# Causal attention with a three-way maxout FFN on one core: high and low halves of the probabilities in one interleaved tile, one DMA transpose per query block, and a new list of matmul counts

## The chip, the cores and the metric

The kernel runs on one core of a Trainium2 chip. Its time is the device time of one execution in microseconds (us). Three runs of the kernel before gave 855.0, 856.35 and 856.51; the median, 856.35, is the time that the changed kernel is compared with. Engines are named as in the profile: PE is TensorE (PEld its weight loads), DVE is VectorE, ACT is ScalarE, POOL is GpSimd, SP is SyncE, which here only issues DMAs.

## The reference, cut to what matters

Eight batches, eight heads, 576 tokens, head size 64. Attention is causal with a bias from a running sum, and its output goes through a maxout FFN:

```python
scores = scale * np.matmul(q, k.transpose(0, 1, 3, 2))
cum = np.cumsum(np.maximum(s, 0.0), axis=-1)
bias = -(cum[:, :, :, None] - cum[:, :, None, :])
scores = np.where(causal, -1000000000.0, scores + np.minimum(bias, 0.0))
attn = np.exp(scores - np.max(scores, axis=-1, keepdims=True))
attn = attn / (np.sum(attn, axis=-1, keepdims=True) + 1e-09)
x = np.matmul(attn, v)          # -> tokens x 512
h = np.maximum(np.maximum(x @ w1, x @ w2), x @ w3)      # 512 -> 768
out = h @ w_out                                          # 768 -> 512
```

## The kernel before, in words

Two heads (j = 0, 1) are worked on together; four such pairs make a batch. The 576 queries of a pair are cut into blocks 0 to 3 of 128 and block 4 of 64 (there the two heads share one tile of 128 rows). A *step* is one block of one pair; 160 steps follow one another. Steps 0 to 15 are blocks 0 and 1 of the first two batches, steps 16 to 39 their blocks 2, 3 and 4, and steps 40 to 159 take the other six batches, five blocks a pair.

Numbers that need more than 16 bits of precision are held as a high half (the value rounded to f16) and a low half (what is left). In step t:

- `scores` (L430, L443, L473, L490) makes the scores of step t+2 on PE in one of two PSUM tiles `s`. It can start only when step t has finished reading its own tile.
- `highest` (L513 or L518, DVE) takes the row maximum, `expo` (L535, ACT) the exponentials and their sums, `inverse` (L548, DVE) 1/sum.
- `probs` makes the high half on ACT (L592, tile `prh`) and the low half on DVE (L595, tile `prl`), the last reader of `s`. For steps 0 to 7 PE transposes both halves through PSUM (L600). In all later steps SP issues DMA transposes: blocks 0 to 3 one of `prh` into `ph` and one of `prl` into `pl` (L607), block 4 two of each (L614). `prh` and `prl` have two buffers each, so the high half of step t+2 waits for the transposes of step t.
- `values` (L674) multiplies with v a step later: 12 matmuls (`av`) for blocks 0 and 1 of a pair, 28 for blocks 2 to 4. They stand on PE ahead of the scores of the next step but one, first all that read `ph`, then those that read `pl`.

The FFN is cut into groups of matmuls: 18 groups of 12 (L810, tile `pm`) and 4 of 18 (L853, tile `po`) for each half of a batch, 256 or 320 tokens wide. A group can be issued when the attention output of that half batch is made. Groups wait in a queue, and from step 10 the list `PLAN` says how many FFN matmuls are issued in each step: the first number ahead of the scores of step t+2, the second behind them. The numbers are upper limits: where the queue is empty, `run_some` issues nothing.

```python
        if fine:
            run_some(PLAN[t - FINE][0])
        ...
        if t + 2 < len(steps):
            scores(t + 2)
        ...
        if fine:
            run_some(PLAN[t - FINE][1])
        ...
        if due:
            values(*due.pop(0))
```

All loads of q, k and v from step 16 on, the output stores and the transposes stand in one queue on SP, in program order.

Of the kernel before, what the change touches and what calls it, by code (L numbers as in the profile page):

```python
# [8 lines left out]
F32 = mybir.dt.float32  # L9
F32R = mybir.dt.float32r  # L10
F16 = mybir.dt.float16
# [10 lines left out]
def kernel(  # L22
# [9 lines left out]
    nc = tc.nc  # L32

    P = 128
    D = 64
    B, NP, _, QKV = qkv.shape
    HB, S = s.shape
# [8 lines left out]
    Q4 = 4 * P  # L46
# [5 lines left out]
    PH = [(0, 256), (256, 320)]  # L52
# [3 lines left out]
    NSEC = 0.417  # L56
    FINE = 10
    PLAN = [
# [13 lines left out]
    ]  # L72

    const = ctx.enter_context(tc.tile_pool(name="const", bufs=1))
# [1 line left out]
    io = ctx.enter_context(tc.tile_pool(name="io", bufs=1))  # L76
    att = ctx.enter_context(tc.tile_pool(name="att", bufs=2))
# [4 lines left out]
    ps_m = ctx.enter_context(tc.tile_pool(name="ps_m", bufs=3, space=PSUM))  # L82
# [118 lines left out]
    def load_w(i, dma=None):  # L201
# [12 lines left out]
        out=tri, in_=tri, pattern=[[-1, P]], compare_op=ALU.is_ge, fill=NEG, base=0, channel_multiplier=1  # L214
# [23 lines left out]
    identh = att.tile([P, P], F16, tag="q4", name="identh")  # L238
# [17 lines left out]
    def cumulate(part):  # L256
        c0, c1, a0, a1 = CUT[part]
        if part == 0:
            C["r"] = io.tile([HB, S], F32, tag="rv1", name="r_t")
            C["c"] = att.tile([HB, S], F32, tag="pTh1", name="c_t", bufs=1)  # L260
            C["cc"] = att.tile([HB, 2, S], F32R, tag="pTl1", name="cc", bufs=1)
            C["cn"] = const.tile([HB, 2, 6], F32R, name="cn")
        r, c, cc, cn = (C[x] for x in ("r", "c", "cc", "cn"))
        w = slice(c0, c1)
        if part == 0:
            nc.vector.tensor_scalar(out=r[:, w], in0=s_t[:, w], scalar1=0.0, scalar2=None, op0=ALU.max)
        nc.vector.tensor_tensor_scan(
            out=c[:, w], data0=r[:, w], data1=r[:, w], initial=c[:, c0 - 1:c0] if part else 0.0,
            op0=ALU.add, op1=ALU.max,
        )  # L270
        if part == 0:
            nc.vector.tensor_copy(out=cc[:, 0, w], in_=c[:, w])
        else:
            nc.scalar.activation(out=cc[:, 0, w], in_=c[:, w], func=AF.Copy)
        eng = nc.gpsimd if part else nc.vector
        eng.tensor_tensor(out=cc[:, 1, w], in0=c[:, w], in1=cc[:, 0, w].bitcast(F32), op=ALU.subtract)
        cf = cc.bitcast(F32)
        for a, x in (
            (slice(0, 2), slice(64, 2 * P, P)), (slice(2, 4), slice(2 * P + 64, Q4, P)),
            (slice(4, 6), slice(Q4 + 32, Q4 + 34)),  # L280
        ):
            if a0 <= a.start < a1:
                eng.tensor_scalar(out=cn[:, :, a], in0=cf[:, :, x], scalar1=-1.0, scalar2=None, op0=ALU.mult)

    C = {}
# [264 lines left out]
    PT = {}  # L550
    TP = {}

    def turned(t):
        tp, pT, m, i = TP.pop(t)
        for c in range(2):
            to, of = pT[c][:, 0:2 * m, i:i + P], tp[:, c, 0:2 * m, :]
            if c and t >= 2 * NP - 2:
                nc.vector.tensor_copy(out=to, in_=of)
            else:
                nc.scalar.activation(out=to, in_=of, func=AF.Copy)  # L560

    def probs(t):

        v, qb = steps[t]
        ps, nm, nk = U.pop(t)
        if t not in RI:
            inverse(t)
        se, nj = SE.pop(t)
        ph = 0 if qb < 2 else 1
        if qb in (0, 2):  # L570
            PT[v, ph] = [
                att.tile([P, (4 + 4 * ph, 4 + 6 * ph)[c], PH[ph][1]], F16, tag=f"pT{'hl'[c]}{ph}", name=f"p{'hl'[c]}{t}", bufs=1)
                for c in range(2)
            ]
        pT = PT[v, ph]
        ri = RI.pop(t)
        halves = [att.tile([P, 8, P], F16, tag=f"pr{c}", name=f"pr{c}{t}") for c in "hl"]
        if nj == 2:
            m = qb + 1
            i = (qb - 2 * ph) * P  # L580
            hv, lv = (x[:, 0:2 * m, :].rearrange("p (m j) c -> p m j c", j=2) for x in halves)
            sets = [
                (hv[:, :, j, :], lv[:, :, j, :], ps[:, j].rearrange("p (m c) -> p m c", c=P), ri[:, j:j + 1])
                for j in range(2)
            ]
        else:
            tail = halves[1][:, 4, :]
            hv, lv = (x[:, 0:4, :] for x in halves)
            src = ps[:, 0:Q4].rearrange("p (m c) -> p m c", c=P)
            sets = [(hv, lv, src, ri[:, 0:1]), (tail[:, 0:D], tail[:, D:P], ps[:, Q4:S], ri[:, 0:1])]  # L590
        for hi, lo, src, sc in sets:
            nc.scalar.activation(out=hi, in_=src, func=AF.Copy, scale=sc)  # L592
        yield
        for hi, lo, src, sc in sets:
            nc.vector.scalar_tensor_tensor(out=lo, in0=src, scalar=sc, in1=hi, op0=ALU.mult, op1=ALU.subtract)  # L595
        if v < NP:
            tp = ps_m.tile([P, 512], F32, tag="m", name=f"tp{t}").bitcast(F16).rearrange("p (c n k) -> p c n k", c=2, k=P)
            for c in range(2):
                for n in range(2 * m):
                    nc.tensor.transpose(out=tp[:, c, n, :], in_=halves[c][:, n, :], identity=identh)  # L600
                if c == 0:
                    for f, a in between.get(t, ()):
                        f(*a)
            TP[t] = (tp, pT, m, i)
        elif nj == 2:
            for c in range(2):
                nc.sync.dma_start_transpose(  # L607
                    out=pT[c][:, 0:2 * m, i:i + P], in_=halves[c][:, 0:2 * m, :].rearrange("p n c -> p (n c)")
                )
        else:  # L610
            for c in range(2):
                n = 4 + c
                for j in range(2):
                    nc.sync.dma_start_transpose(  # L614
                        out=pT[c][:, 0:2 * n, 256:320].rearrange("p (n j) c -> p n j c", j=2)[:, :, j, :],
                        in_=halves[c][j * D:(j + 1) * D, 0:n, :].rearrange("p n c -> p (n c)"),
                    )
        yield


# [34 lines left out]
    def values(v, ph):  # L655
        b, g, _ = visits[v]
        r = R[v]
        nq = PH[ph][1]
        pT = PT.pop((v, ph))
# [3 lines left out]
        for t in range(2):  # L663
            for kb in range(min(blocks[-1] + 1, 4)):
                c0 = max(kb - blocks[0], 0) * P
                for vt in ("vh", "vl")[:2 - t]:
                    for j in range(2):
                        todo.append((j, r[vt][:, j, kb, :], pT[t][:, 2 * kb + j, c0:nq], c0))
        if ph:
            for vt in ("vh", "vl"):  # L670
                for j in range(2):
                    todo.append((j, r[vt][:, j, 4, :], pT[1][:, 8 + j, 256:320], 2 * P))
        for n, (j, lt, rt, c0) in enumerate(todo):
            nc.tensor.matmul(  # L674
                av[j * D:(j + 1) * D, c0:nq], lhsT=lt, rhs=rt,
# [246 lines left out]
    todo = {}  # L922
# [253 lines left out]
```

## Time and profile before

| | |
|---|---|
| median of three runs | 856.35 us |
| profiled execution | 857.01 us, of which the span of instructions is 855.2 us |
| PE busy | 816.1 us (95%), granted clock 0.993 over the span |
| DVE, ACT, POOL busy | 555.9, 556.9, 417.1 us (65%, 65%, 49%) |
| DMA transposes | 368, in one queue with the loads and stores |

PE is busy nearly throughout, so the time is PE's work plus PE's idle time. The span begins with an attention stage in which the FFN queue is still short, and ends with FFN work alone. Matmuls overlap, and the duration of a single one is longer than the distance to the next; the rate is read from merged rows (so many matmuls in so many us).

### The profile page before, as it was taken

How to read it: one execution, taken by the hardware profiler on the slowest of the kernel's cores; microseconds unless marked ns; L12 is line 12 of the kernel's file. 1: busy time of each engine (PE TensorE's matmuls, PEld its weight loads, DVE VectorE, ACT ScalarE, POOL GpSimd, SP SyncE). 2: the span in 40 equal slices, each digit the busy share in tenths (PEclk: the TensorE clock that was granted, in tenths of full speed). 3: DMA queues.
4: the chain of work that ended last, by engine and by line, in shares of the span. 5: the costliest groups of instructions: out<-in, count | busy, mean ns of one | idle time of the engine just before them, and what ended most of it. 6: DMA issues, size and time to landing. Idle time of an engine off the chain costs nothing. (4 is left out here: it accounts for less than half of the span.)

```text
span 855.2 us, 19957 instructions
## 1 busy us (share of the span) xinstructions
PE 816.1 (95%) x7100; PEld 639.7 (75%) x7100; DVE 555.9 (65%) x1451; ACT 556.9 (65%) x1493; POOL 417.1 (49%) x621
## 2 busy tenths in 40 slices
PE   4988899997999999999999999999999999999998
PEld 3766677765677778777887788777887788777875
DVE  8978979676778667676766676666756675661110
ACT  4767768776687777777777676777766676651111
POOL 6513523234545657664756757464656656221221
PEclk9989999999999999999999999999999999999999
DMA  9823745896777686868777686657847565321000
GB/s 354 338 73 80 140 109 124 175 183 146 154 174 164 157 153 147 173 133 168 150 166 156 147 178 150 140 134 154 162 131 153 129 155 136 92 66 45 19 9 31
DMA packets 233668, 120.76 MB, mean 141 GB/s; under 512 B 209376, under 2 KB 218208, under 8 KB 233568
## 3 DMA queue, kind: packets, MB, share of 16 engines
q1 hardware_dynamic: 232416, 117.65, 60.2%
q10 hardware_dynamic: 1152, 1.84, 0.6%
q8 instruction: 56, 0.92, 0.5%
q14 instruction: 44, 0.36, 0.2%
HBM read 60.18 MB, written 9.44 MB: 81 GB/s over the span
## 5 line engine op out<-in xcount | busy, mean ns | idle before, releaser
L810 PE MATMUL pm<-x,w 128*128 128x256 f16 (+1 forms) x3456 | 456.6, 287 | 4.7 <-DVE x L684 2.8
L810 PEld LDWEIGHTS <-w 128*128 128x128 f16 x3456 | 326.9, 98 | 98.5 <-issue 12.7
L818 POOL CAST hh<-m 128x256 f16<-128x256 f32 (+1 forms) x96 | 50.2, 523 | 296.0 <-DVE m L829 227.5
L595 DVE SCALAR_TENSOR_TENSOR prl<-s,ri,prh 128x512 f16<-128x512 f32 (+3 forms) x288 | 152.7, 567 | 48.2 <-ACT prh L592 27.5
L592 ACT ACTIVATE prh<-s,ri 128x512 f16<-128x512 f32 (+3 forms) x288 | 141.7, 538 | 64.2 <-DVE ri L548 58.1
L535 ACT ACTIVATE s<-s,nm 128x512 f32<-128x512 f32 (+4 forms) x288 | 151.2, 525 | 24.9 <-DVE nm L513 14.4
L829 DVE SCALAR_TENSOR_TENSOR m<-pm,m 128x256 f32<-128x256 f32 (+1 forms) x192 | 87.1, 454 | 116.4 <-PE pm L810 94.1
L853 PE MATMUL po<-hh,w 128*128 128x256 f16 (+1 forms) x768 | 149.9, 287 | 0.0
L513 DVE CUSTOM_DVE_ANT_0 s<-s,later 128x128 f32<-128x128 f32 (+4 forms) x216 | 113.8, 527 | 43.1 <-PE s L430 23.7
L853 PEld LDWEIGHTS <-w 128*128 128x128 f16 x1152 | 109.5, 98 | 28.7 <-issue 1.7
L853 PE MATMUL po<-hl,w 128*128 128x320 f16 (+1 forms) x384 | 109.9, 286 | 0.0
L826 ACT ACTIVATE m<-pm 128x256 f32<-128x256 f32 (+1 forms) x96 | 38.8, 404 | 59.5 <-PE pm L810 57.4
L819 POOL TENSOR_TENSOR hl<-m,hh 128x256 f16<-128x256 f32 (+1 forms) x96 | 72.6, 757 | 7.8
L185 POOL TENSOR_TENSOR l<-raw,h 64x576 fp32r<-64x576 f32 x48 | 67.5, 1407 | 6.8 <-ACT h L172 5.9
L177 POOL TENSOR_TENSOR h<-raw,h 64x640 fp32r<-64x640 f32 x40 | 61.6, 1539 | 15.6 <-ACT h L168 15.0
L863 ACT ACTIVATE o<-po,os 128x256 f32<-128x256 f32 (+1 forms) x64 | 31.9, 499 | 55.5 <-PE po L853 54.7
L674 PEld LDWEIGHTS <-vh 128*64 128x64 f16 x832 | 45.3, 109 | 24.1 <-issue 18.0
L683 ACT ACTIVATE x<-av 128x256 f16<-128x256 f32 (+1 forms) x64 | 26.3, 410 | 54.4 <-PE av L674 54.3
L535 ACT ACTIVATION_READ_ACCUMULATOR s<-s,nm 128x1 f32 x288 | 57.2, 199 | 0.0
L430 PE MATMUL s<-h 128*128 128x128 f32 (+1 forms) x192 | 56.3, 369 | 0.8 <-ACT s L535 0.8
L155 POOL CAST l<-kb 64x576 fp32r<-64x576 f32 x48 | 32.8, 684 | 46.5 <-PE s L443 45.8
L548 DVE RECIPROCAL ri<-se 128x2 f32<-128x2 f32 (+1 forms) x160 | 25.4, 159 | 39.9 <-ACT se L540 39.2
(155 smaller groups left out, 1117.5 us busy)
## 6 DMA issues: line engine op xcount, KB each, us to landing
raw<-in_qk_dram SPq DMA_DIRECT2D x48, 608.0 KB, 4.4
r<-in_w_dram SPq DMA_DIRECT2D x24, 512.0 KB, 10.2
rv<-in_qkv_dram SPq DMA_DIRECT2D x32, 320.0 KB, 3.5
out_dram<-o SPq DMA_DIRECT2D x32, 160.0 KB, 2.0
out_dram<-o SPq DMA_DIRECT2D x32, 128.0 KB, 1.9
raw<-in_qkv_dram SPq DMA_DIRECT2D x8, 480.0 KB, 4.1
ph<-prh SPq DMA_TRANSPOSE x184, 3.0
pl<-prl SPq DMA_TRANSPOSE x184, 2.8
```

The costliest lines, as they stand in the source:

```text
L177: (nc.vector if v < 5 * NP else nc.gpsimd).tensor_tensor(out=h[own, 0:QP], in0=raw[own, 0:QP], in1=h[own, 0:QP].bitcast(F32), op=ALU.subtract)
L185: nc.gpsimd.tensor_tensor(out=l[far, QP:V0], in0=raw[far, QP:V0], in1=h[far, QP:V0].bitcast(F32), op=ALU.subtract)
L430: nc.tensor.matmul(ps[:, j, :nk], lhsT=w[:, qs], rhs=w[:, QP:QP + nk], start=(x == "h"), stop=(x == "l"), skip_group_check=True,)
L513: nc.vector.tensor_tensor_reduce(out=of, in0=of, in1=mask, scale=-SCALE, scalar=3.0e38, op0=ALU.add, op1=ALU.min, accum_out=nm[:, j:j + 1],)
L535: nc.scalar.activation(out=sc, in_=sc, func=AF.Exp, bias=nm[:, j:j + 1], scale=-1.0 if below(t) else 1.0, accum_out=sm[:, j:j + 1],)
L592: nc.scalar.activation(out=hi, in_=src, func=AF.Copy, scale=sc)
L595: nc.vector.scalar_tensor_tensor(out=lo, in0=src, scalar=sc, in1=hi, op0=ALU.mult, op1=ALU.subtract)
L810: nc.tensor.matmul(pm[:, :nq], lhsT=w[:, wt, kt, :], rhs=xt, start=(n == 0), stop=(n == 3 * NKT - 1))
L818: nc.gpsimd.tensor_copy(out=st["hh"][:, ft, :nq], in_=m1[:, :nq])
L819: nc.gpsimd.tensor_tensor(out=st["hl"][:, ft, :nq], in0=m1[:, :nq], in1=st["hh"][:, ft, :nq], op=ALU.subtract)
L829: nc.vector.scalar_tensor_tensor(out=m1[:, :nq], in0=pm[:, :nq], scalar=HSC, in1=m1[:, :nq], op0=ALU.mult, op1=ALU.max)
L853: nc.tensor.matmul(pm[:, :nq], lhsT=W[18 + ft][:, wt, dt, :], rhs=st[ht][:, ft, :nq], start=(n == 0), stop=(n == 3 * NFT - 1),)
```

## The change

**Tiles.** `prh` and `prl` become one tile `pr` of 16 blocks of 128 columns; for key block k it holds the high half of both heads, then the low half of both heads. `ph` and `pl` become one tile `pT` in the same order. Blocks 0 to 3 of a pair get one DMA transpose of twice the length, block 4 two (one for each head's 64 rows) in place of four: 184 transposes in place of 368, with the same data. In steps 0 to 7 the PE transposes are the same in number and order. The matmuls of `values` are the same, in the same order; all of them now read `pT`. The tile of the running sum (`c`) moves to another pool.

**The list.** `PLAN` is made anew.

```diff
     PLAN = [
-        (15, 0), (18, 12), (18, 12), (11, 1), (17, 16), (18, 12), (12, 0), (13, 17), (18, 12), (9, 0), (18, 9), (10, 14),
+        (24, 0), (18, 12), (18, 12), (19, 0), (17, 16), (18, 12), (18, 0), (9, 21), (19, 11), (15, 0), (14, 13), (12, 12),
 ...
@@ def probs(t):
-            PT[v, ph] = [
-                att.tile([P, (4 + 4 * ph, 4 + 6 * ph)[c], PH[ph][1]], F16, tag=f"pT{'hl'[c]}{ph}", name=f"p{'hl'[c]}{t}", bufs=1)
-                for c in range(2)
-            ]
+            PT[v, ph] = att.tile([P, 8 + 10 * ph, PH[ph][1]], F16, tag=f"pT{ph}", name=f"pt{t}", bufs=1)
         pT = PT[v, ph]
         ri = RI.pop(t)
-        halves = [att.tile([P, 8, P], F16, tag=f"pr{c}", name=f"pr{c}{t}") for c in "hl"]
+        pr = att.tile([P, 16, P], F16, tag="pr", name=f"pr{t}")
         if nj == 2:
-            hv, lv = (x[:, 0:2 * m, :].rearrange("p (m j) c -> p m j c", j=2) for x in halves)
+            both = pr[:, 0:4 * m, :].rearrange("p (m c j) k -> p m c j k", c=2, j=2)
             sets = [
-                (hv[:, :, j, :], lv[:, :, j, :], ps[:, j].rearrange("p (m c) -> p m c", c=P), ri[:, j:j + 1])
+                (both[:, :, 0, j, :], both[:, :, 1, j, :], ps[:, j].rearrange("p (m c) -> p m c", c=P), ri[:, j:j + 1])
                 for j in range(2)
             ]
 ...
         elif nj == 2:
-            for c in range(2):
-                nc.sync.dma_start_transpose(
-                    out=pT[c][:, 0:2 * m, i:i + P], in_=halves[c][:, 0:2 * m, :].rearrange("p n c -> p (n c)")
-                )
+            nc.sync.dma_start_transpose(
+                out=pT[:, 0:4 * m, i:i + P],
+                in_=pr[:, 0:4 * m, :].rearrange("p n c -> p (n c)"),
+            )
         else:
-            for c in range(2):
-                n = 4 + c
-                for j in range(2):
-                    nc.sync.dma_start_transpose(
-                        out=pT[c][:, 0:2 * n, 256:320].rearrange("p (n j) c -> p n j c", j=2)[:, :, j, :],
-                        in_=halves[c][j * D:(j + 1) * D, 0:n, :].rearrange("p n c -> p (n c)"),
-                    )
+            for j in range(2):
+                nc.sync.dma_start_transpose(
+                    out=pT.rearrange("p (k j) q -> p k j q", j=2)[:, :, j, 256:320],
+                    in_=pr[j * D:(j + 1) * D, 0:9, :].rearrange("p n c -> p (n c)"),
+                )
```

What the new list does on PE is read from the order of its instructions. Up to the scores of step 23 nothing moves. After that these are the FFN matmuls that stand between the scores of the step before and the scores of the step named (the largest differences):

```
ahead of the scores of step   24  27  30  32  33  35  36  39  42  44 | 57  58  59  60
before                        24  23  24  35  21  19  23  22  21  26 | 23  18  22  26
now                           33  31  30  40  26  25  30  29  24  30 | 13   0   0  21
```

At the scores of step 56 the new order has issued 55 FFN matmuls more than the old one, at those of step 60 as many. After that the two stay within 10 matmuls of each other.

On PE, at the scores of step 58 (`s`, four of 512 columns) in the kernel before; `po_1_2` is an FFN group, `w` its weights:

```order
L853 LDWEIGHTS w_2026
L853 MATMUL po_1_2_4596<-hh_1_3932,w_2026 128x320
L430 MATMUL s_4606<-h_0_3997 128x512
L430 MATMUL s_4606<-h_1_4194 128x512
L430 MATMUL s_4606<-l_0_3998 128x512
L430 MATMUL s_4606<-l_1_4195 128x512
L853 LDWEIGHTS w_2026
L853 MATMUL po_1_2_4596<-hh_1_3932,w_2026 128x320
```

The same place on PE in the changed kernel; `av` is the product with v of the pair before, `s_4500` the scores of step 58, `s_4527` those of step 59:

```order
L672 LDWEIGHTS vl_4081
L672 MATMUL av_1_4461<-pt_4234,vl_4081 64x64
L430 MATMUL s_4500<-h_0_3939 128x512
L430 MATMUL s_4500<-h_1_4135 128x512
L430 MATMUL s_4500<-l_0_3940 128x512
L430 MATMUL s_4500<-l_1_4136 128x512
L443 MATMUL s_4527<-h_0_3939 128x256
L443 MATMUL s_4527<-h_1_4135 128x256
```

No FFN matmul stands any more from the scores of step 57 to the `av` behind those of step 59; the queue is empty there.

On SP, from the load of a head (`raw`) in step 32 to the first transposes of step 34, before:

```order
L139 DMA raw_0_2852<-in_qk_dram 128x1216
L607 DMA_TRANSPOSE ph_2806<-prh_2883 128x8x128
L607 DMA_TRANSPOSE pl_2807<-prl_2884 128x8x128
L614 DMA_TRANSPOSE ph_2806<-prh_2954 128x4x64 x2
L614 DMA_TRANSPOSE pl_2807<-prl_2955 128x5x64 x2
L607 DMA_TRANSPOSE ph_3021<-prh_3023 128x6x128
L607 DMA_TRANSPOSE pl_3022<-prl_3024 128x6x128
```

And the same stretch of SP in the changed kernel, up to the load behind the first transpose of step 34:

```order
L139 DMA raw_0_2814<-in_qk_dram 128x1216
L606 DMA_TRANSPOSE pt_2763<-pr_2845 128x16x128
L612 DMA_TRANSPOSE pt_2763<-pr_2914 128x9x64 x2
L606 DMA_TRANSPOSE pt_2975<-pr_2976 128x12x128
L127 DMA rv_3028<-in_qkv_dram 128x640
```

Eight issues became four; each now stands behind the low half, where the one of `prh` stood behind the high half alone.

## Rows read from the trace of the kernel before

**Rows 1.** Busy us (x instructions) by stage; last three columns: PE clock, DMA share, GB/s.

```profile
0.00:130.00 130.00, 107.21 (x945) 83.53 (x945) 107.86 (x250) 87.66 (x249) 55.19 (x90) 0.96 0.61 183
130.00:262.00 132.00, 121.54 (x1064) 91.77 (x1060) 98.69 (x210) 96.13 (x241) 53.24 (x79) 1.00 0.75 159
262.00:760.00 498.00, 496.48 (x4356) 393.66 (x4355) 330.90 (x953) 355.94 (x967) 291.82 (x424) 1.00 0.67 146
760.00:856.00 96.00, 90.84 (x744) 70.76 (x742) 18.42 (x42) 17.13 (x39) 16.85 (x30) 0.99 0.12 33
```

**Rows 2.** PE's waits from 130 to 262 us: total, times, longest.

```profile
PE av L674 <- DMA pl<-prl: 3.9, 4, 2.2
PE s L490 <- DVE prl L595: 3.5, 4, 1.4
PE s L490 <- DVE am L342: 1.1, 1, 1.1
PE s L443 <- DVE prl L595: 1.0, 1, 1.0
PE s L430 <- ACT s L535: 0.8, 1, 0.8
```

**Rows 3.** Chain that ended last: start, us, what (its FFN matmuls alone).

```profile
781.14 23.58 PE pm L810 x216
...
812.72 29.34 PE pm L810 x216
```

**Rows 4.** Timeline, steps 32 to 39: start, us, engine, what, [idle before and releaser].

```profile
188.68 2.48 SPq L614 DMA_TRANSPOSE ph<-prh  x2
...
191.27 2.49 SPq L614 DMA_TRANSPOSE pl<-prl  x2
...
192.31 0.36 PE L490 MATMUL s<-qkh 128*128 128x256 f32 x1 [1.08 <-DVE prl L595]
...
196.23 0.65 PE L674 MATMUL av<-pl,vh 128*64 128x320 f16 x8 [1.35 <-DMA pl<-prl]
...
213.25 0.65 PE L674 MATMUL av<-pl,vh 128*64 128x320 f16 x8 [2.21 <-DMA pl<-prl]
```

**Rows 5.** Waits of the whole span: total, times, longest.

```profile
ACT prh L592 <- DMA ph<-prh: 5.3, 4, 2.8
...
PE av L674 <- DMA pl<-prl: 4.9, 5, 2.2
```

**Rows 6.** Transposes of line L607: issue on SP, ns min/median/max; issue to landing.

```profile
L607 SPq DMA_TRANSPOSE pl<-prl x120: 1167/1220/4210, 58.3 to 765.8; - x120
...
DMA to landing us min/median/max: 2.3/3.0/6.6
```

**Rows 7.** Scores of step 56 to those of step 60, columns as in Rows 1.

```profile
286.07:304.35 18.28, 17.47 (x151) 13.10 (x150) 11.44 (x30) 13.91 (x37) 11.42 (x17) 1.00 0.75 173
```

**Rows 8.** Timeline of that stretch: low halves of steps 56, 58; scores 58; FFN.

```profile
292.03 0.88 DVE L595 SCALAR_TENSOR_TENSOR prl<-s,ri,prh 128x256 f16<-128x256 f32 x2
...
294.60 0.74 PE L430 MATMUL s<-h 128*128 128x512 f32 x2
...
301.44 1.41 DVE L595 SCALAR_TENSOR_TENSOR prl<-s,ri,prh 128x512 f16<-128x512 f32 x2 [0.67 <-ACT prh L592]
...
303.24 1.36 PE L810 MATMUL pm<-x,w 128*128 128x256 f16 x11 [0.81 <-DVE x L684]
```

**Rows 9.** PE idle, and the granted clock behind it, columns as in Rows 1.

```profile
50.00:52.00 2.00, 0.34 (x4) 0.17 (x3) 1.90 (x9) 1.32 (x4) 0.77 (x2) 1.00 0.34 41
52.00:54.00 2.00, 1.78 (x12) 1.27 (x12) 0.45 (x2) 1.94 (x8) 1.54 (x3) 0.51 0.55 221
54.00:56.00 2.00, 2.00 (x16) 1.36 (x16) 1.64 (x4) 0.83 (x3) 0.00 (x0) 0.63 0.03 8
211.00:213.25 2.25, 0.04 (x2) 0.00 (x0) 0.60 (x1) 0.48 (x1) 1.06 (x1) 1.00 0.79 268
213.25:216.00 2.75, 2.75 (x28) 2.21 (x27) 2.07 (x4) 1.97 (x5) 0.00 (x0) 1.00 0.92 150
```

More of the change, by code (lines that the diff above doesn't have):

```diff
@@ L259, in cumulate @@
             C["r"] = io.tile([HB, S], F32, tag="rv1", name="r_t")
-            C["c"] = att.tile([HB, S], F32, tag="pTh1", name="c_t", bufs=1)
-            C["cc"] = att.tile([HB, 2, S], F32R, tag="pTl1", name="cc", bufs=1)
+            C["c"] = io.tile([HB, S], F32, tag="rv2", name="c_t")
+            C["cc"] = att.tile([HB, 2, S], F32R, tag="pT1", name="cc", bufs=1)
             C["cn"] = const.tile([HB, 2, 6], F32R, name="cn")
@@ L555, in turned @@
         for c in range(2):
-            to, of = pT[c][:, 0:2 * m, i:i + P], tp[:, c, 0:2 * m, :]
+            to = pT[:, 0:4 * m, i:i + P].rearrange("p (m c j) q -> p m c j q", c=2, j=2)[:, :, c]
+            of = tp[:, 0:4 * m, :].rearrange("p (m c j) k -> p m c j k", c=2, j=2)[:, :, c]
             if c and t >= 2 * NP - 2:
@@ L586, in probs @@
         else:
-            tail = halves[1][:, 4, :]
-            hv, lv = (x[:, 0:4, :] for x in halves)
+            both = pr[:, 0:8, :].rearrange("p (m c) k -> p m c k", c=2)
             src = ps[:, 0:Q4].rearrange("p (m c) -> p m c", c=P)
-            sets = [(hv, lv, src, ri[:, 0:1]), (tail[:, 0:D], tail[:, D:P], ps[:, Q4:S], ri[:, 0:1])]
+            sets = [
+                (both[:, :, 0, :], both[:, :, 1, :], src, ri[:, 0:1]),
+                (pr[:, 8, 0:D], pr[:, 8, D:P], ps[:, Q4:S], ri[:, 0:1]),
+            ]
         for hi, lo, src, sc in sets:
@@ L596, in probs @@
         if v < NP:
-            tp = ps_m.tile([P, 512], F32, tag="m", name=f"tp{t}").bitcast(F16).rearrange("p (c n k) -> p c n k", c=2, k=P)
+            tp = ps_m.tile([P, 512], F32, tag="m", name=f"tp{t}").bitcast(F16).rearrange("p (n k) -> p n k", k=P)
             for c in range(2):
-                for n in range(2 * m):
-                    nc.tensor.transpose(out=tp[:, c, n, :], in_=halves[c][:, n, :], identity=identh)
+                for n in (4 * k + 2 * c + j for k in range(m) for j in range(2)):
+                    nc.tensor.transpose(out=tp[:, n, :], in_=pr[:, n, :], identity=identh)
                 if c == 0:
@@ L605, in probs @@
         elif nj == 2:
-            for c in range(2):
+            nc.sync.dma_start_transpose(
+                out=pT[:, 0:4 * m, i:i + P],
+                in_=pr[:, 0:4 * m, :].rearrange("p n c -> p (n c)"),
+            )
+        else:
+            for j in range(2):
                 nc.sync.dma_start_transpose(
-                    out=pT[c][:, 0:2 * m, i:i + P], in_=halves[c][:, 0:2 * m, :].rearrange("p n c -> p (n c)")
-                )
-        else:
-            for c in range(2):
-                n = 4 + c
-                for j in range(2):
-                    nc.sync.dma_start_transpose(
-                        out=pT[c][:, 0:2 * n, 256:320].rearrange("p (n j) c -> p n j c", j=2)[:, :, j, :],
-                        in_=halves[c][j * D:(j + 1) * D, 0:n, :].rearrange("p n c -> p (n c)"),
-                    )
+                    out=pT.rearrange("p (k j) q -> p k j q", j=2)[:, :, j, 256:320],
+                    in_=pr[j * D:(j + 1) * D, 0:9, :].rearrange("p n c -> p (n c)"),
+                )
         yield
@@ L667, in values @@
                     for j in range(2):
-                        todo.append((j, r[vt][:, j, kb, :], pT[t][:, 2 * kb + j, c0:nq], c0))
+                        todo.append((j, r[vt][:, j, kb, :], pT[:, 4 * kb + 2 * t + j, c0:nq], c0))
         if ph:
@@ L671, in values @@
                 for j in range(2):
-                    todo.append((j, r[vt][:, j, 4, :], pT[1][:, 8 + j, 256:320], 2 * P))
+                    todo.append((j, r[vt][:, j, 4, :], pT[:, 16 + j, 256:320], 2 * P))
         for n, (j, lt, rt, c0) in enumerate(todo):
```

24 rows, old and new, of the table PLAN are left out of this document.

## The prediction

> **What bounds the kernel now.** I read the table of busy time by stage first. PE is idle 22.8 us up to 130 us, 10.5 from 130 to 262, 1.5 from 262 to 760 and 4.4 after that, and at full clock from 130 us on [rows 1]. From 262 us the kernel is PE's work and nothing else. The change neither adds nor takes away a matmul, so the time can only move through PE's idle time, and up to the scores of step 23 (about 130 us) the order on PE is as it was. What can be won is therefore the 10.5 us of steps 24 to 49 and about 1 us at the end; everything else can only be lost. The waits say who ends the 10.5 us [rows 2]: 6.4 us are scores that wait for their PSUM tile or its chain (3.5 + 1.1 + 1.0 + 0.8), 3.9 us are `av` matmuls that wait for the transposes of the low half. One FFN matmul costs PE 23.58 / 216 = 0.109 us at 256 columns and 29.34 / 216 = 0.136 us at 320 [rows 3].
>
> **Filler ahead of the scores.** Where PE waits for the attention chain, the scores start no earlier with more filler ahead of them, but the FFN matmuls moved there cost nothing. Steps 24 and 30 get 9 and 6 matmuls of 256 columns more, 0.98 and 0.65 us, inside waits of 1.4 and 1.1. Steps 42 and 44 get 3 and 4 of 320, 0.41 and 0.54, inside 0.8 and 1.0. For steps 33, 36 and 39, which with step 24's 1.4 make up the 3.5 us, the extra matmuls are as long as the waits or longer (7 of 320 are 0.95 us; step 36 waits 1.08 [rows 4] and has 6 more a step earlier), so all of 3.5 - 1.4 = 2.1 us goes. Sum: 0.98 + 0.65 + 0.41 + 0.54 + 2.1 = 4.7 us. Bounds: 0 if the filler only pushes the chain, 6.4 if the chain gains as well. I take -4.7.
>
> **Transposes.** An issue takes SP 1.22 us, and a transfer lands 3.0 us after its issue begins [rows 6]. At step 33 four issues follow each other from 188.68 to 193.76, and `av` waits until 196.23 [rows 4]. Now there are two, behind the low half. The merged issue and its landing stand in no row: the issue lies between 1.2 (as now) and 2.4 us (two of now), the landing between 2.3 and 4.2 us (3.0 and one issue more). I take 1.3 and 3.4, near the single issue, since its median barely differs from its minimum over tiles of 2 to 8 blocks. Two issues of 2.5 us together go from the path, so the wait of 1.35 us all but goes. In return the part of `av` that read the high half, about 1.0 us of PE work, cannot run ahead any more, so of the 2.21 us at 213.25 some 1.0 stays. With the two small waits that is 1.2 + 1.2 + 0.3: I take -2.7, between 0 and -3.9. At the end of the attention the same wait is 4.9 - 3.9 = 1.0 us [rows 2, 5], and ten more FFN matmuls now stand ahead of it in that step: -0.8, between 0 and -1.0.
>
> The Trainium skill (DMA: Bandwidth & Descriptors, Issuing engines are not separate DMA queues) holds that the time a sequencer takes to start a DMA is usually small beside the DMA itself. Here it is 1.22 of 3.0 us; by the page's rule this term would be near nothing and the sum 2.7 us longer.
>
> **What is paid for it.** At the scores of step 56 the new order has 55 matmuls more behind it, 55 x 0.136 = 7.5 us. They are missing in steps 56 to 59, where the queue is empty. Before, these four steps took 18.28 us with PE busy 17.47 [rows 7]; now PE has 10.0 us of work there, and the attention chain sets the pace. Its length is read from the same steps. From the scores of step 56 (286.07) to the end of its low half (292.91) are 6.84 us, then come the scores of step 58; from those (294.60) to the end of their low half (302.85) 8.25 us, then the scores of step 60 [rows 7, 8]: 15.1 us. On PE the 21 matmuls ahead of step 60 also wait for the output of `av`, as they do now at 303.24, and 12 or so of 0.109 us follow that wait: 16.0 us in all. Bounds for these four steps: 11.4 us, DVE's busy time there [rows 7], and 18.3 as now. With 16.0 the stretch gets only 2.3 us shorter for 7.5 us of work taken out of it: +5.2 us (bounds +0.6 and +7.5).
>
> The PE idles twice there, for about 1.6 and 2.9 us. In the trace an idle stretch of this length was once followed by a fallen clock: from 50 to 52 us PE is busy 0.34 us at full clock, and in the next four us the granted clock is 0.51 and 0.63, mostly the lower of the two levels (1.2 of 2.4 GHz); but after the 2.2 us at 211 it stays at 1.00 [rows 9]. At the price of that fall, (0.49 + 0.37) x 2 = 1.7 us, and an even chance, +0.9 us. The Trainium skill (TensorE: Matmul & The Clock Gate, HAM oscillation) says that PE falls back to its slow clock when it is left idle between bursts, which makes the next burst pay; by that alone the term is +1.7, and the row at 211 us shows an idle stretch that did not.
>
> **Later steps.** From step 61 to 159 PE waits 1.5 us in all [rows 1], so there is next to nothing to win. The new list takes up to 10 matmuls (1.4 us) from ahead of single scores and puts them behind, at about a dozen steps; a chain that just kept up then shows as a wait of some tenths. No row has it: between 0 and 3.5 us (12 x 0.3), I take +1.5.
>
> **Sum.** -4.7 - 2.7 - 0.8 + 5.2 + 0.9 + 1.5 = -0.6 us against the profiled execution, 857.01 us (855.2 of span and 1.8 around it): 856.4. That execution lies 0.66 above the median of the three runs, so against the median of 856.35 I say 855.7. Written with x for the length of steps 56 to 59, the sum is x - 17.5, and x is 16.0 + 0.9 in it.
>
> **Rivals.**
> *The stalls go and the empty queue costs little.* All 6.4 + 3.9 + 1.0 us of waits go, the later steps cost 0.3, the clock stays up, and the four steps take 16.0: -11.3 + 0.3 + 5.2 = -5.8, so 850.6 against the median. For it: both edits attack just these waits. Against it: scores held by the chain are held by DVE and ACT, which do the same work.
> *The empty queue decides (slower).* Steps 57 to 59 are left to a chain with PE idle; the chain gets no shorter than it was, and the clock falls: x = 18.3 + 1.7 = 20.0, sum +2.5, so 858.9 against the median; with 3.5 for the later steps 860.9. It decides for slower from x = 19.2 on. For it: ACT is busy 13.9 of 18.3 us there already [rows 7]. Against it: with fewer FFN evictions ACT and DVE are freer.
> *The one tile holds the chain.* The high half of step t+2 now waits for both halves' transposes of step t, where it waited for those of `ph` alone; that was already 5.3 us in four places [rows 5], all before 215 us where loads crowd the queue. If each becomes 1 us longer and the scores follow, it is +4 on the -0.6: 859.8. Against it: with half the issues the merged transfer should land no later than the second of now.
>
> **Chances.** The forecast 0.46 (its own range 853.7 to 857.9), the stalls gone 0.27, the empty queue 0.20, the one tile 0.07. A change under 0.2%, 1.7 us, cannot be told from none here. Of the forecast's 0.46, 0.09 is faster and 0.04 slower than that. Faster: 0.27 + 0.09 = 0.36; the same: 0.33; slower: 0.20 + 0.07 + 0.04 = 0.31. The range, 851.0 to 860.0, leaves out the far ends of the two large rivals.
>
> **What would show it.** In the profile after: PE's waits before the scores of steps 24 to 44 should sum to about 1.7 us, those of `av` for transposes to about 1.2. Between the scores of steps 56 and 60 there should be 16 to 17 us with PE busy about 10 to 11, and two idle stretches of 1.5 to 3 us ahead of the scores of steps 58 and 59, with DVE's low half as releaser. The issue of a merged transpose should be near 1.3 us. I am wrong in the main term if the four steps take under 14 or over 18.3 us, in the second if `av` still waits 3 us or more, and in the last if PE idles more than 4 us from 310 to 760 us.

## The result

Slower by 0.7%: the changed kernel took 861.95 us (four runs, 861.72 to 862.32) against 856.13 for the kernel before in the same comparison. The ratio is 1.0071 (95% interval 1.0053 to 1.0088). Timed again, with six runs, it was 1.0063 (1.0039 to 1.0087). The forecast was no change, with slower at 0.31; the time lies above the range.

Up to the scores of step 23 both traces run alike (129.14 and 129.28 us), so everything below is counted from there to the end of the span: 726.1 us before, 730.8 after. The table of busy time by stage after, which answers [rows 1] (stage, length, then busy us and instructions of PE, PEld, DVE, ACT, POOL, last PE clock, DMA share, GB/s):

```profile
0.00:130.00 130.00, 106.76 (x943) 83.42 (x945) 108.11 (x250) 87.52 (x249) 54.63 (x90) 0.96 0.57 182
130.00:262.00 132.00, 126.50 (x1101) 95.91 (x1098) 97.91 (x209) 95.57 (x238) 55.26 (x81) 0.99 0.74 158
262.00:760.00 498.00, 490.80 (x4277) 388.79 (x4277) 331.01 (x948) 354.44 (x960) 288.37 (x419) 0.99 0.66 146
```

PE idles 5.5 us from 130 to 262 us, where it was 10.5: half of it is won. From 262 to 760 it idles 7.2 us, where it was 1.5. The sum of PE's busy time grew as well, by 3.7 us (816.1 to 819.8) for the same matmuls: the granted clock fell twice behind step 23. Cut at the same steps in both kernels, first before, then after (scores of step 23 to those of 45, to those of 60, to the end):

```profile
129.14:239.64 110.50, 100.23 (x889) 76.11 (x888) 81.82 (x165) 79.64 (x196) 44.89 (x65) 1.00 0.74 156
239.64:304.35 64.71, 63.70 (x530) 47.45 (x529) 48.40 (x128) 50.61 (x137) 36.08 (x53) 1.00 0.78 169
304.35:855.23 550.88, 545.78 (x4751) 433.30 (x4748) 318.08 (x910) 339.78 (x917) 281.71 (x417) 1.00 0.57 125
```

```profile
129.28:242.18 112.90, 107.40 (x942) 81.99 (x941) 81.73 (x165) 81.21 (x202) 45.25 (x65) 0.98 0.73 156
242.18:306.08 63.90, 59.45 (x477) 44.12 (x476) 46.98 (x128) 49.00 (x132) 35.10 (x53) 0.95 0.71 163
306.08:860.06 553.98, 546.89 (x4751) 433.59 (x4748) 320.95 (x910) 340.80 (x917) 282.31 (x417) 1.00 0.56 125
```

53 matmuls moved from the second stretch to the first. The groups keep their order, and both kernels are through with the first groups of 256 columns by step 33, so what the first stretch has more is 53 of 320 columns: 53 x 0.136 = 7.2 us of work by [rows 3]. The first stretch got 2.4 us longer for it, the second only 0.8 us shorter, and the third, with the same matmuls, 3.1 us longer: +4.7. Of the third's 3.1 us, 2.0 are idle time of PE; for 1.1 us more PE was busy at full clock with the same matmuls, and why stays open.

PE's waits from 130 to 262 us after (total, times, longest), for [rows 2]:

```profile
PE s L490 <- DVE pr L595: 3.3, 3, 2.2
PE s L490 <- DVE am L342: 0.7, 1, 0.7
PE pm L808 <- ACT m L824: 0.7, 1, 0.7
PE av L672 <- DMA pt<-pr: 0.5, 1, 0.5
```

The `av` waits fell from 3.9 to 0.5 us. The waits of the scores of steps 24 to 44 fell from 6.4 to 4.4 us only, where 1.7 was forecast. The worst, 2.23 us at step 39, is a chain in the timeline, for [rows 4] (start, us, engine, what, idle before and releaser):

```profile
199.80 0.52 SPq L127 DMA_DIRECT2D rv<-in_qkv_dram  x1
...
200.37 0.45 SPq L139 DMA_DIRECT2D raw<-in_qk_dram  x1
...
200.94 4.65 SPq L606 DMA_TRANSPOSE pt<-pr  x1
...
209.87 1.05 ACT L592 ACTIVATE pr<-s,ri 128x384 f16<-128x384 f32 x2 [4.89 <-DMA pt<-pr]
...
210.95 1.14 DVE L595 SCALAR_TENSOR_TENSOR pr<-s,ri,pr 128x384 f16<-128x384 f32 x2 [3.62 <-ACT pr L592]
...
212.24 0.36 PE L490 MATMUL s<-qkh 128*128 128x256 f32 x1 [2.23 <-DVE pr L595]
```

SP's issue of step 35's transpose, right behind two loads, takes 4.65 us. It lands at about 209.8, and only then can ACT write step 37's high half, because both halves now share the tile under transposition. DVE and PE follow. The hold is not new: before the change the second transpose of step 35 took 4.21 us to issue (the maximum in [rows 6]), and ACT waited 2.8 us for the first one's landing ([rows 5]). Over the whole span this wait of ACT, for [rows 5], is now

```profile
ACT pr L592 <- DMA pt<-pr: 17.3, 13, 4.9
...
PE av L672 <- DMA pt<-pr: 2.4, 3, 1.0
```

where it was 5.3 us in 4. The merged issue and its landing, for [rows 6], are near what I took (1.3 and 3.4 us) in the median, and far from it when held:

```profile
L606 SPq DMA_TRANSPOSE pt<-pr x120: 1188/1387/4709, 58.5 to 769.6; - x120
...
DMA to landing us min/median/max: 2.3/3.4/8.8
```

Last, the starved steps 56 to 59, for [rows 7], and the granted clock behind the two long idle stretches, for [rows 9]:

```profile
288.70:306.08 17.38, 12.93 (x96) 9.67 (x95) 10.46 (x29) 14.62 (x41) 7.48 (x12) 0.80 0.70 173
210.00:212.00 2.00, 0.01 (x1) 0.00 (x0) 1.05 (x2) 2.00 (x5) 0.40 (x1) 1.00 0.81 207
212.00:214.00 2.00, 1.76 (x11) 1.53 (x13) 1.64 (x5) 1.94 (x6) 0.32 (x1) 0.73 0.27 112
214.00:216.00 2.00, 2.00 (x19) 1.48 (x20) 1.94 (x3) 1.31 (x3) 1.76 (x2) 0.50 0.00 0
298.00:300.00 2.00, 0.57 (x3) 0.60 (x4) 1.28 (x4) 1.71 (x6) 0.00 (x0) 0.57 0.63 190
300.00:302.00 2.00, 2.00 (x11) 1.63 (x12) 0.44 (x2) 1.22 (x3) 0.51 (x1) 0.50 0.85 192
```

Steps 56 to 59 took 17.4 us (18.28 before) for 7.5 us of work taken out. PE waits three times there, each time for the low half of two steps earlier:

```profile
292.01 0.59 PE L430 MATMUL s<-h 128*128 128x384 f32 x2 [0.79 <-DVE pr L595]
...
295.49 0.70 PE L430 MATMUL s<-h 128*128 128x512 f32 x2 [0.88 <-DVE pr L595]
...
299.43 0.77 PE L443 MATMUL s<-h 128*128 128x256 f32 x2 [2.78 <-DVE pr L595]
```

### The profile page after: what moved, and what is told of

Same layout as the page of the kernel before. It is cut to its first block, busy times and chain, and to the rows that moved or that the text cites. A ratio compares the mean times of both kernels' runs of the same rounds, so it can differ in the third digit from the quotient of the medians.

```text
span 860.1 us, 19642 instructions
## 1 busy us (share of the span) xinstructions
PE 819.8 (95%) x7100; PEld 642.5 (75%) x7100; DVE 557.6 (65%) x1451; ACT 557.8 (65%) x1493; POOL 416.7 (48%) x621
## 3 DMA queue, kind: packets, MB, share of 16 engines
q10 hardware_dynamic: 1152, 1.84, 0.7%
## 4 chain that ended last, share of the span: by engine, by line
PE 76%; DMA 5%; ACT 1%; DVE 1%; issue 1%; POOL 0%; SPq 0%; ACTq 0%; POOLq 0%
PE pm L808 42%; PE po L851 15%; PE av L672 8%; PE s L430 6%; DMA pt<-pr 5%; PE s L443 3%; PE s L490 1%; PE s L473 1%; DVE pr L595 1%; ACT pr L592 1%; ACT s L535 0%; DMA out_dram<-o 0%; ACT o L861 0%; POOL l L185 0%; PE s L464 0%
## 5 line engine op out<-in xcount | busy, mean ns | idle before, releaser
L592 ACT ACTIVATE pr<-s,ri 128x512 f16<-128x512 f32 (+3 forms) x320 | 148.6, 516 | 79.3 <-DVE ri L548 60.4
L595 DVE SCALAR_TENSOR_TENSOR pr<-s,ri,pr 128x512 f16<-128x512 f32 (+3 forms) x320 | 158.9, 538 | 57.1 <-ACT pr L592 56.5
L513 DVE CUSTOM_DVE_ANT_0 s<-s,later 128x128 f32<-128x128 f32 (+4 forms) x216 | 113.7, 527 | 23.1 <-PE s L443 8.7
L672 PE MATMUL av<-pt,vh 128*64 128x320 f16 (+4 forms) x832 | 78.4, 273 | 2.5 <-DMA pt<-pr 2.4
```

Source lines behind the costliest of these rows:

```text
L513: nc.vector.tensor_tensor_reduce(out=of, in0=of, in1=mask, scale=-SCALE, scalar=3.0e38, op0=ALU.add, op1=ALU.min, accum_out=nm[:, j:j + 1],)
L672: nc.tensor.matmul(av[j * D:(j + 1) * D, c0:nq], lhsT=lt, rhs=rt, start=(n < 2), stop=(n >= len(todo) - 2), skip_group_check=True,)
```

## The experiments

Over six to twelve runs the kernels' times scatter by 2 to 7 us, part of it in the opening steps (the scores of step 23 begin between 126.9 and 129.3 us). So each is read twice: by its ratio to the kernel before, and by its profile from the scores of step 23, cut at the same steps, with PE's idle time in brackets (in the last stretch up to PE's last matmul, 3.4 us ahead of the end). The two readings differ by up to 2.8 us (e6), and there is one profile of each kernel but the changed one, so a difference of 2 us between two profiles alone is weak evidence:

| kernel | ratio (95%) | 23 to 45 | 45 to 60 | 60 to end | sum |
|---|---|---|---|---|---|
| before | 1 | 110.5 (10.3) | 64.7 (1.0) | 550.9 (1.7) | 726.1 |
| changed | 1.0071 (1.0053 to 1.0088) | 112.9 (5.5) | 63.9 (4.5) | 554.0 (3.7) | 730.8 |
| changed again | 1.0063 (1.0039 to 1.0087) | 112.4 (6.4) | 64.2 (4.4) | 553.6 (3.4) | 730.2 |
| e1 tiles alone | 0.9986 (0.9970 to 1.0002) | 107.0 (8.0) | 65.3 (1.5) | 551.3 (1.7) | 723.5 |
| e2 list alone | 1.0054 (1.0034 to 1.0075) | 112.8 (6.2) | 65.9 (7.0) | 552.4 (2.7) | 731.2 |
| e3 changed, third tile | 0.9992 (0.9976 to 1.0008) | 108.6 (3.1) | 64.0 (4.5) | 553.8 (3.4) | 726.4 |
| e4 changed, list spread | 1.0019 (1.0005 to 1.0033) | 113.7 (7.8) | 61.1 (3.6) | 554.5 (3.9) | 729.3 |
| e5 tiles, late list | 1.0011 (0.9992 to 1.0029) | 107.0 (8.0) | 65.2 (1.5) | 553.6 (3.3) | 725.8 |
| e6 changed, pad matmuls | 1.0040 (1.0021 to 1.0059) | 115.2 (7.9) | 63.0 (2.0) | 554.1 (3.7) | 732.3 |
| e7 tiles, third tile | 0.9938 (0.9915 to 0.9961) | 106.0 (7.1) | 65.4 (1.6) | 551.6 (1.8) | 723.0 |
| e8 changed, load on ACT | 1.0032 (1.0012 to 1.0052) | 109.7 (4.5) | 66.0 (7.2) | 553.5 (3.2) | 729.1 |
| e9 e7, load on ACT | 0.9941 (0.9920 to 0.9962) | 105.4 (6.5) | 65.2 (1.3) | 551.8 (2.1) | 722.4 |
| e10 e7, few early | 0.9935 (0.9913 to 0.9957) | 102.5 (1.4) | 65.4 (3.4) | 551.2 (1.8) | 719.1 |

**Which half of the change (e1, e2).** The changed kernel with the old numbers, and the kernel before with the new ones:

```diff
-        (24, 0), (24, 0), (24, 0), (34, 0), (34, 0), (34, 0), (34, 0), (24, 15), (20, 10), (9, 3), (22, 11), (18, 9),
+        (24, 0), (24, 0), (24, 0), (24, 0), (25, 0), (25, 0), (25, 0), (24, 15), (20, 10), (9, 3), (22, 11), (18, 9),
...
```

> The merged tiles and transposes of the change, with the list of the kernel before. Theory T (the merged tile itself costs time: a high half must wait for the whole transpose of two steps ago, which lands later): 857 to 859.5, ACT's waits for transposes 12 us or more (5.3 in the kernel before, 17.3 in the changed one), scores of steps 33 to 39 later by 1 us or more. Theory L (the list costs the time, the tiles win their av waits of 3.4 us): 852 to 854.

> Separate tiles and transposes as in the kernel before, with the new list. Theory L: 859.5 to 862.5, with PE idle about 4 us in steps 56 to 59, the clock fallen behind it, and some 2 us of idle in later steps. Theory T: the filler ahead of the scores of steps 24 to 44 now gains its 4.7 us, the starved steps cost at most that: 855 to 858.

The tiles alone are 2.6 us shorter by the profile (the ratio leaves no change possible; on the scale of the first comparison it is 854.9 us, between the two forecasts); the list alone is 5.1 us longer and 1.0054 (860.8, as L said). The list by itself makes the kernel slower, and the tiles by themselves do not. In e2, PE idles 7.0 us in steps 56 to 59 in place of the expected 4: `av` waits 2.51 us there for its transposes, a wait that the merged tiles spare. ACT's waits for transposes are there in e1 too, as T said:

```profile
ACT pr L592 <- DMA pt<-pr: 13.8, 10, 3.7
```

PE pays for them: its waits before the scores of steps 36 and 39 are 1.69 and 1.81 us, where they were 1.08 and 0.77. It gets back more, since the `av` waits up to step 45 (3.7 us) are gone. The two halves do not add up: +5.1 and -2.6 give 2.5, and both together gave 4.7.

**The shared tile under the new list (e3).**

```diff
-        pr = att.tile([P, 16, P], F16, tag="pr", name=f"pr{t}")
+        if 17 < t < 39 and t % 3 == 0:
+            pr = att.tile([P, 16, P], F16, tag="pT0", name=f"pr{t}", bufs=1)
+        else:
+            pr = att.tile([P, 16, P], F16, tag="pr", name=f"pr{t}")
```

> The changed kernel, with every third probability tile of steps 18 to 36 in the space of the block-0/1 transposes, which is idle in these steps: no high half waits for a transpose of two steps ago there. Theory T: PE's wait of 2.23 us before the scores of step 39 falls under 0.8, so do those of steps 30 to 36, no fallen clock at 212 us: 857 to 859. Theory L: the waits fall but the scores come no earlier: 861 to 862.

4.4 us shorter, and back at the kernel before (0.9992; 855.4 on the first comparison's scale, a little below T's range). The issue is held as before, but nothing waits for it; the scores of steps 36 and 39 start without a wait and the clock at 212 us stays up. One wait in T's list stayed, 1.51 us before step 31. Step 39:

```profile
200.05 4.97 SPq L609 DMA_TRANSPOSE pt<-pr  x1
...
208.86 0.39 PE L490 MATMUL s<-qkh 128*128 128x256 f32 x1
```

So the shared tile costs some 4 us under the new list. What the 53 early matmuls (7.2 us) add to the first stretch says it too: 2.3 us on separate tiles (before to e2), 2.6 with a third tile (e7 to e3), 5.9 on two shared tiles (e1 to changed). The last is the best known: e1 and e5 have the same instructions there and took 107.0 each, and those of the changed kernel stand in four profiles, 112.4 to 115.2 (e4 and e6 have them up to step 45), so it is 5.4 to 8.2. Nearly 5 us are hidden in the first two cases, under 2 in the last. Under the old list the profiles show only 0.5 us for the third tile (e1 to e7), but the ratios show 0.5%, 4 us, with intervals apart (0.9986 to 0.9938): e1's profile is that of its fastest run of twelve, at a granted clock of 0.999 where their median is 0.9935, and what its usual run pays is not in it.

**The starved steps (e4, e6).** e4 gives the 53 matmuls back evenly from step 45 on (shown is the row of the list for steps 46 to 57; the three entries ahead of it change too); e6 leaves the list and fills PE's idle time ahead of the scores of steps 57 to 59 with matmuls that count for nothing.

```diff
-        (9, 15), (7, 11), (21, 6), (17, 10), (6, 7), (9, 15), (7, 11), (14, 13), (14, 13), (10, 2), (13, 11), (24, 0),
+        (12, 9), (10, 5), (16, 6), (10, 13), (5, 3), (11, 11), (8, 5), (14, 9), (8, 14), (5, 3), (13, 9), (9, 5),
```

```diff
+    IDLE = {55: 6, 56: 6, 57: 22}
...
+        if t in IDLE:
+            pad = ps_m.tile([P, 512], F32, tag="m", name=f"pad{t}")
+            for n in range(IDLE[t]):
+                nc.tensor.matmul(
+                    pad[:, 0:256], lhsT=identb, rhs=identb.unsqueeze(1).to_broadcast([P, 2, P]),
+                    start=True, stop=True, skip_group_check=True,
+                )
         if t + 2 < len(steps):
             scores(t + 2)
```

> The changed kernel with its list mended between steps 45 and 59: the 53 FFN matmuls taken early are given back evenly, two to five per step, so that the queue isn't empty at steps 57 to 59; the list is as changed elsewhere. Theory L: idle of 4.45 us in steps 56 to 59 falls under 1.0, no fallen clock at 300 us: 855.5 to 857.5. Theory T: the attention chain is held in steps 45 to 59 anyway and the idle time moves into them: 859.5 to 862.

> The changed kernel with matmuls that count for nothing (6, 6 and 22 of 256 columns into a spare PSUM tile) ahead of the scores of steps 57, 58 and 59, where PE stands idle 0.8, 0.9 and 2.8 us. Theory C (the fallen clock behind the idle time is a cost of its own): granted clock 1.00 from 299 to 306 us, the four steps 56 to 59 take 15.0 to 15.6 us in place of 17.4, 728 to 729 from step 23 to the end. Theory D (the chain sets the pace there, the clock with it costs nothing): 17.0 to 17.6 us and 730.5 to 731.

e4 is 2.8 us shorter than the changed kernel from step 45 to 60 (61.1 against 63.9), with the clock at 1.00, and its ratio is 0.4 to 0.5% lower. But PE still idles 3.6 us there, now spread out:

```profile
PE s L430 <- DVE pr L595: 1.4, 2, 1.1
PE s L443 <- DVE pr L595: 1.3, 2, 1.1
PE pm L808 <- DVE x L682: 0.8, 1, 0.8
```

Neither theory was right alone: the chain holds PE in these steps even so, and hollowing out four of them costs another 2.8 us. In e6 the clock stayed up and the four steps took 16.46 us in place of 17.38:

```profile
289.64:306.10 16.46, 14.50 (x131) 11.14 (x129) 10.46 (x29) 14.52 (x41) 7.41 (x12) 1.00 0.82 180
```

So the clock is worth some 0.9 us there, between C and D. Profiles of the same steps with the whole fall of 6.8 us took 17.4 to 17.7 us (changed twice, e3), and one with half of it 17.06 (e8). PE's work alone is slower by more, about 2.1 us by an estimate (12.93 us busy, against 14.50 less 34 x 0.109 in e6), so the chain covers the rest. (e6's sum, 732.3, is above both forecasts: its first stretch is 2.3 us longer than the changed kernel's with the same instructions in it, which bounds what one profile can tell of that stretch.)

**The late steps (e5).** e1 with the old list up to the scores of step 60 and the new one behind; the first row that differs (steps 58 to 69):

```diff
-        (21, 9), (22, 14), (6, 9), (17, 16), (16, 8), (24, 12), (18, 18), (10, 8), (15, 15), (15, 9), (24, 9), (15, 12),
+        (21, 9), (21, 15), (4, 11), (14, 19), (15, 9), (24, 12), (15, 21), (5, 13), (11, 19), (15, 9), (24, 9), (12, 15),
...
```

> The merged tiles, the list of the kernel before up to the scores of step 60 and the new list behind them. From the scores of step 23 to the end of the span the kernel before took 726.1 us, the changed one 730.8, the tiles with the old list 723.5. Theory E (all of the list's cost lies in steps 23 to 59): 723.5 to 724.5. Theory S (it is split, some 3 us of it in the later steps): 725.5 to 727, with PE idle 1.3 us near step 89 where FFN groups wait for POOL.

Theory S holds: 2.3 us over e1, all behind step 60. On merged tiles all seven profiles with the new list there took 553.5 to 554.5 us, the four with the old one 551.2 to 551.8. Its waits from 395 to 440 us:

```profile
PE po L851 <- POOL hh L816: 0.8, 1, 0.8
PE av L672 <- DMA pt<-pr: 0.6, 1, 0.6
PE po L851 <- POOL hl L817: 0.5, 1, 0.5
```

Between the scores of steps 89 and 90 the new list has 40 FFN matmuls where 33 stood. They come to the products of `hh` and `hl` before POOL has made these, and 1.3 us are lost. Behind the scores of step 82 `av` comes before its transposes.

**What holds the transposes (e8).**

```diff
-        nc.sync.dma_start(out=t, in_=qk[b, g, j])
+        (nc.scalar if v < 19 else nc.sync).dma_start(out=t, in_=qk[b, g, j])
```

> The changed kernel with the first loads of the six later batches (pairs 16 to 18, from step 31 to 43) issued on ACT's queue, not on SP's ahead of the transposes. If a transpose is held 4.7 us because SP's queue has the load of 608 KB in front of it: issues of transposes at steps 32 to 36 fall to 1.6 us, PE's wait before the scores of step 39 from 2.2 to under 0.8 us, no fallen clock at 212 us, 726 to 728.5 from step 23 to the end. If the DMA engines themselves are taken up: issues still 3 us or more and 730 to 731.5.

In between. The issues fell from 4.7 to 2.9 us, not to 1.6, and that was enough for step 39's scores to start without a wait:

```profile
183.17 2.95 SPq L606 DMA_TRANSPOSE pt<-pr  x1
...
197.76 2.90 SPq L606 DMA_TRANSPOSE pt<-pr  x1
```

But the queue is not what holds them. In both places ACT had issued its load about 5 us earlier. Where it issued one at the same time, the hold is as long as ever, on another queue:

```profile
211.91 0.53 SPq L127 DMA_DIRECT2D rv<-in_qkv_dram  x1
...
212.54 5.25 SPq L606 DMA_TRANSPOSE pt<-pr  x1
212.59 0.33 ACTq L139 DMA_DIRECT2D raw<-in_qk_dram  x1
```

So it is at 236.92 (5.62 us), and the two holds end in PE's waits of 1.84 and 2.08 us before the scores of steps 42 and 47. The 2.9 us that are left go with the other load, `rv` of 320 KB, which stands just ahead on SP in both places: over all eleven profiles with merged tiles, issues of 16 blocks just behind `rv` alone took 2.7 to 3.5 us (34 places), just behind `rv` and `raw` 4.2 to 5.0 (18). Those just behind `raw` alone, all of 8 blocks, took 1.23 to 1.25 (28). So SP's queue is not the cause; the hold goes with the loads that were issued around that time on either queue, and what they hold it by is not shown. In the sum 1.7 us are won: the first stretch is 3.2 us shorter, the second, with the later of these two waits in it, 2.1 longer.

**Towards a better version (e7, e9, e10).** e7 is e1 with e3's edit, e9 adds e8's. e10 adds to e7 19 early matmuls, in place of 53, and gives them back one or two per step:

```diff
-        (15, 0), (18, 12), (18, 12), (11, 1), (17, 16), (18, 12), (12, 0), (13, 17), (18, 12), (9, 0), (18, 9), (10, 14),
-        (9, 0), (13, 14), (11, 13), (9, 0), (14, 13), (18, 9), (12, 0), (15, 9), (17, 1), (18, 9), (17, 10), (9, 3),
-        (15, 9), (13, 5), (21, 6), (14, 13), (9, 3), (13, 11), (13, 5), (18, 9), (13, 14), (9, 3), (15, 9), (13, 5),
+        (24, 0), (18, 12), (18, 12), (11, 1), (17, 16), (18, 12), (18, 0), (13, 17), (18, 12), (9, 0), (18, 9), (10, 14),
+        (9, 0), (13, 14), (11, 13), (9, 0), (14, 13), (18, 9), (12, 0), (15, 9), (21, 1), (18, 9), (15, 10), (8, 3),
+        (14, 9), (12, 5), (19, 6), (12, 13), (8, 3), (12, 11), (11, 5), (17, 9), (11, 14), (8, 3), (14, 9), (12, 5),
```

> The merged tiles, the list of the kernel before, and a third probability tile in steps 18 to 36. With the old list the tiles alone took 723.5 us from the scores of step 23 to the end, PE idle 3.5 us ahead of the scores of steps 36 and 39. If the tile that is still being transposed holds the chain there: those waits under 1 us, 720.5 to 722. If the chain is late for another reason: 723 to 724.

> The merged tiles, the list of the kernel before, the third probability tile in steps 18 to 36, and the first loads of the later batches on ACT's queue. The third tile took 723.0 us from the scores of step 23 to the end, with 1.5 us of PE idle at the scores of step 36 and 1.0 at the av behind step 39. If those are still transposes held behind a load: both under 0.5 us, 720.5 to 721.8. If they come from the chain of DVE and ACT: 722.5 to 724.

> The merged tiles and the third tile with the list of the kernel before, but 9, 6 and 4 FFN matmuls moved ahead of the scores of steps 24, 30 and 44, less than those wait, and given back one or two per step from 45 to 58, so that the queue never runs empty. Theory F (a matmul inside a wait costs nothing as long as what it is taken from has slack): 2.0 us less than the third tile alone, 720.7 to 721.5 from the scores of step 23 to the end. Theory G (the attention chain sets the pace of all steps 23 to 59, what is filled early is idle later): 722.5 to 723.5.

All three beat both kernels by their ratios. e7: the waits of steps 36 and 39 are gone, as forecast, but an `av` at 191.8 us now waits 1.5 us for its transposes, and 723.0 lies at the edge of the other range. e9: that wait goes, others come (the scores of step 44, 0.97 to 1.51 us, and 0.42 new before step 43), 0.6 us in all. e10 is the shortest by the profile, 3.9 us below e7 where F gave 2.0. Its three stretches:

```profile
128.57:231.12 102.55, 101.11 (x908) 77.95 (x907) 81.55 (x165) 80.61 (x199) 47.06 (x65) 1.00 0.74 168
231.12:296.53 65.41, 62.05 (x509) 45.70 (x510) 47.41 (x128) 49.38 (x134) 35.32 (x53) 1.00 0.78 161
296.53:847.68 551.15, 546.01 (x4751) 433.97 (x4748) 318.29 (x910) 340.18 (x917) 281.41 (x417) 1.00 0.55 126
```

908 matmuls in 102.5 us, where e7 had 889 in 106.0. PE idles 5.6 us less. The waits that were filled (steps 24, 30, 44) gave 3.1 of that, less 1.0 in waits that came new; the others (3.6 us, among them the `av` behind step 36 and the scores of steps 40 and 42) went too, which I did not foresee and have not explained. The second stretch gave nothing back (65.4 with 19 matmuls less): there G was right. By their ratios e7, e9 and e10 cannot be told apart (0.9938, 0.9941, 0.9935), so e10's 3.9 us stand in one profile only.

**The changed kernel again.**

> The changed kernel itself on the same chip as the two above, with more runs. Its clock falls behind idle stretches of over 2 us may or may not come in an execution. If the profile of the first run is typical: 730 to 732 us from the scores of step 23 to the end, ratio 1.005 to 1.009. If it was an unlucky one: 727 to 729, ratio 1.002 to 1.005.

730.2 and 1.0063: the first profile was typical.

## Why the prediction was wrong

By its own steps, changed against before from the profiles:

| stretch | forecast | measured |
|---|---|---|
| scores 23 to 56: 55 matmuls more, +7.5, less 4.7 and 2.7 | +0.1 | +2.5 |
| scores 56 to 60, x with the clock | 16.9 for 18.28: -1.4 | 17.4: -0.9 |
| scores 60 to end: +1.5 and -0.8 | +0.7 | +3.1 |
| sum | -0.6 | +4.7 |

Of the 5.3 us between the two sums, 2.4 lie ahead of step 56 and 2.4 behind step 60.

- **"For steps 33, 36 and 39 ... the extra matmuls are as long as the waits or longer ... so all of 3.5 - 1.4 = 2.1 us goes": this step failed.** It treated the waits as fixed gaps to be filled. They went from 2.1 to 2.9 us, step 39's from 0.77 to 2.23, and the filler term as a whole took 2.0 us from the score waits (6.4 to 4.4), not 4.7. What ends the long ones is a transpose that lands late. On separate tiles (e2) step 39's wait grew too, to 2.19 us, and there DVE waits for the low half's transpose of two steps before:

```profile
206.61 1.05 ACT L592 ACTIVATE prh<-s,ri 128x384 f16<-128x384 f32 x2 [2.23 <-DMA ph<-prh]
...
210.02 1.14 DVE L595 SCALAR_TENSOR_TENSOR prl<-s,ri,prh 128x384 f16<-128x384 f32 x2 [3.57 <-DMA pl<-prl]
```

Where the chain did not wait for the held transpose (e3), or this one was held less (e8), step 39's wait was gone with the same filler ahead of it. Why the landing came later behind the filler, on separate tiles too, is not shown.
- **The -4.7 and the -2.7 were added as if independent.** From the scores of step 23 to those of 56 each came out by itself: the list alone +2.4 us (7.5 - 4.7 = 2.8 forecast, e2), the tiles alone -3.0 (-2.7, e1). Together they gave +2.5, not +0.1. That the list's sum fits is luck: it took 2.9 us from the `av` waits (3.7 to 0.8 up to step 45) and only 1.2 from the score waits (6.4 to 5.2), and the `av` waits are what the tiles win as well (3.7 to 0), so both terms spent the same wait. With both, the held transpose stands on the path of the scores besides. I had this as the rival "the one tile holds the chain" at 0.07, with the right mechanism (ACT's wait, 5.3 to 17.3 us). e3 shows its worth under the new list: 4.3 us in that stretch, the clock at 212 us among it. It was priced as +4, and with too small a chance: its rows showed such waits of ACT of up to 2.8 us [rows 5] and issues of up to 4.2 us [rows 6] before anything was merged. That a merged transfer "should land no later" did not hold where it was held (8.8 us from issue to landing).
- **The starved steps held.** 16.0 + 0.9 forecast, 17.4 measured; the idle stretches stand before the scores of steps 58 and 59 with DVE's low half as releaser (0.88 and 2.78 us; a third, 0.79, before step 57's). That the clock's +0.9 is what e6 measured (0.93) is luck: it was half of 1.7 for an even chance, the fall came, and it cost about half of the price; without it the four steps took 16.5, not 16.0. The rival of the empty queue needed x over 19.2 and did not come (on separate tiles, e2, the four steps took 19.4).
- **A second clock fall was not in the sum.** Behind step 39's wait PE ran at the lower level, and steps 39 to 41 took 11.24 us, against 9.66 in the second profile, where the same 2.25 us of wait had no fall behind it: 1.6 us.
- **The later steps were mis-sized and misplaced.** I took +1.5 as tenths at a dozen steps; e5 has 2.3 us, and over half of it (1.3) is one place, where POOL's output is late for PE, which I did not look at. My own test for this step (PE idling more than 4 us from 310 to 760 us) was too loose to catch it: it idles 2.8, nearly all in two places.
- **The last `av` wait (-0.8) stayed**: 0.95 us for 1.00. The ten matmuls more also stand ahead of the work that makes its input; no run tests this.

## What to carry to other kernels

Before filling a wait, ask what ends it. Where a late transpose ended it (steps 36 and 39), filler won nothing; where the chain was free of that (e3), nearly 5 of 7.2 us were hidden. Two edits that go for the same wait cannot both win it, so each of their gains has to be named by its wait. When two buffers become one, every reader of either half holds both; before merging, look for waits on the slowest of the transfers and give the merged buffer one more copy (e3, e7). Work moved early from a shared queue has to be missing somewhere: taking back a little at many steps was 2.8 us better here than all at four (e4).

## What the hardware showed

- The same idle stretch before step 39 (2.2 to 2.4 us) was followed by a fallen clock in two of five profiles (changed and e6; not in e2, e4 and the second of the changed kernel); the 2.8 us before step 59 in all five profiles that have it (changed twice, e2, e3, e8).
- The issue of a merged DMA transpose on SP took 1.19 us in the median for 4 blocks, 1.23 for 8, 1.40 for 12 and 1.61 for 16. For 16 blocks just behind a load of 320 KB (`rv`) it took 2.7 to 3.5 us, just behind that and one of 608 KB (`raw`) 4.2 to 5.0. With the second load issued on ACT's queue at the same time it took 5.25 (e8), so another queue did not help.
- With the same instructions the granted clock of the first 130 us was 0.96 in some profiles and 1.00 in others, and the scores of step 23 began up to 2.4 us apart (126.9 to 129.3).
- Matmuls whose product nobody reads made steps 56 to 59 0.9 us shorter (16.46 us in e6, 17.38 without them).
